# Choosing evacuation engines and the place of the output scaling by a beam search, and packing a short group's chunks two to a bank

## The chip, the cores and the metric

The kernel runs on one core of one Trainium2 chip. The metric is the device time of one execution in microseconds (us); "span" is the time from the first to the last instruction in the profile of one execution, about 2 us less. All runs told of here were with a granted TensorE clock between 0.996 and 1.0. Short names: PE is TensorE's matmul row, PEld its weight loads, DVE is VectorE, ACT is ScalarE, POOL is GpSimd, SP is SyncE.

## The reference, cut to what matters

```python
# x: (4, 12480, 128), inducing: (32, 128), w_in: (128, 2048), w_out: (2048, 128), alpha: (2048,)
def mab(q, kv):                       # attention with softmax, scale 1/sqrt(128)
    a = softmax(scale * (q @ kv.T))
    return a @ kv
h   = mab(inducing, x)                # 32 summary rows for each of 4 batches
y   = mab(x, h)                       # back to all rows; 49,920 rows of 128
u   = y @ w_in
out = (max(u, 0) + alpha * min(u, 0)) @ w_out
```

The kernel uses two identities. `y @ w_in` is (softmax weights) @ (h @ w_in), so the first layer's matmul contracts over 32 and not 128. And max(u,0) + alpha min(u,0) is (1 - alpha) relu(u) + alpha u; the second term is linear, so a small matmul, called here the linear term, adds it to the same accumulator. The softmax division is left to the very end, one scaling of the finished rows.

## The kernel before: the parts that the argument touches

Rows go in groups of 512; a batch has 24 full groups and one short group of 192 rows. A group's second layer accumulates in one of two PSUM banks (`accs`), chosen by the group's parity. The other six PSUM banks are a ring. A group takes four *fills*. Fill j: four matmuls, each on its own 32 rows of TensorE, write four ring banks (128x512); ACT or DVE *evicts* each bank with a relu into the SBUF tile `gt`; one fill later, 16 matmuls (`mm2`) multiply `gt` by the second-layer weights.

```python
    def fill(st, g, j):
        ...
        for r in range(4):
            ps = bank()                                   # next bank of the ring of six
            mm(ps[:, :w], st.hW[32*r : 32*r+32, j, :], rep[32*r : 32*r+32, :w])
            banks.append((ps, (ring_n[0] - 1) % RING))
        if j == 2:
            linear(st, lin_groups(st.b, g))               # even g: for groups g and g+1
        ca, cd = w * 0.75 + 96, w * 1.04 + 68             # modelled ns on ACT, DVE
        ...
        for r, (ps, i) in enumerate(banks):               # greedy: whichever ends first
            ta, td = max(clk["A"], ready) + ca, max(clk["D"], ready) + cd
            if ta <= td: ...  nc.scalar.activation(out=gt[:, r, :w], in_=ps[:, :w], func=RELU)
            else:        ...  nc.vector.tensor_relu(gt[:, r, :w], ps[:, :w])

    def mm2(st, g, j, gt, done):                          # runs after the NEXT fill's matmuls
        ...                                               # 16 matmuls into accs[(st.b*NG + g) % 2]
        if j == NJ - 1 and st.b * NG + g > 0:
            finish(st, g)                                 # the scaling, on DVE

    def linear(st, groups):                               # groups = [g, g+1]
        for k in range(NB):
            for r, g in enumerate(groups):
                mm(accs[(st.b*NG + g) % 2][:pp, k, :], st.rep[g][32*r : ...], st.hA[32*r : ...],
                   start=(r == 1 and k == 0), ...)        # r == 1 restarts the bank of g-1 and g+1
    def finish(st, g):                                    # ob = acc * 1/den, then the output DMA
        ...

    for b, g, j in fills:
        gt, done = fill(states[b], g, j)
        for fn in tasks.pop((b * NG + g, j), []):         # the next batch's work, and this one's
            fn()                                          # b_scores, b_den; most take a ring bank
        if prev is not None:
            mm2(*prev)
        prev = (states[b], g, j, gt, done)
```

So group g-1's last `mm2` comes after fill 0 of group g, its scaling is evicted on DVE during fill 1, and, for even g, the linear term in fill 2 restarts that very bank for group g+1. I call fills 0 to 3 of a group its first to fourth fill.

The softmax here doesn't subtract the row's maximum and nothing guards it: scores larger than these inputs give would overflow.

Of the kernel before, what the change touches and what calls it, by code (L numbers as in the profile page):

```python
# [15 lines left out]
P = 128  # L16
NB = 4
GRP = P * NB
NQ = 4
# [5 lines left out]
def kernel(  # L25
# [62 lines left out]


    clk = {"P": 0.0, "A": 0.0, "D": 0.0}  # L90
    free = [0.0] * RING

    def bank():
        i = ring_n[0] % RING
        ring_n[0] += 1
        clk["P"] = max(clk["P"], free[i])
        return ring[i]

    def spent(e, ns, release=True):
        clk[e] = max(clk[e], clk["P"] + 100) + ns  # L100
        if release:
            free[(ring_n[0] - 1) % RING] = clk[e] + 100
# [82 lines left out]
    def e_xpose_pe(st, u):  # L185
        e1 = st.e1.pop(u)
        tp = bank()[:].bitcast(bf16)
        if u < NS:
            e1T = work.tile([P, NB, P], bf16, name="e1T", tag="e1T")
            for j in range(NB):  # L190
# [3 lines left out]
            pin(nc.vector.tensor_copy(  # L194
                out=e1T[:].rearrange("p j m -> p (j m)"), in_=tp[:, : NB * P]
            ))
# [11 lines left out]
    def a_scores(st, u, by_dma=True):  # L208
# [24 lines left out]
        clk["P"] += 320  # L233
        spent("A", 680)
# [5 lines left out]
    def a_accum(st, u):  # L240
# [3 lines left out]
        clk["P"] += 240  # L244
# [22 lines left out]
        spent("D", 220)  # L267
# [38 lines left out]
    def b_scores(st, s):  # L306
# [16 lines left out]
        clk["P"] += 320  # L323
        spent("A", 490)
# [31 lines left out]
    def b_den(st, s):  # L356
        e2 = st.e2.pop(s)
        ps = bank()
        clk["P"] += 240
        spent("D", 250)  # L360
# [16 lines left out]

    def shape_of(g):
        return (P, NB) if g < NS * NQ else (PR, JR)

    def fill(st, g, j):
        pp, nb = shape_of(g)
        w = pp * nb
# [3 lines left out]
        for r in range(4):  # L387
            ps = bank()
            mm(
                ps[:, :w], st.hW[32 * r : 32 * r + 32, j, :], rep[32 * r : 32 * r + 32, :w]  # L390
            )
            banks.append((ps, (ring_n[0] - 1) % RING))
        if j == 2:
            linear(st, lin_groups(st.b, g))
        ca, cd = w * 0.75 + 96, w * 1.04 + 68
        ready = clk["P"] + 150 + w * 0.42
        clk["P"] = ready - 50 + (240 if j == 2 and lin_groups(st.b, g) else 0)
        done = ready
        for r, (ps, i) in enumerate(banks):
            ta, td = max(clk["A"], ready) + ca, max(clk["D"], ready) + cd  # L400
            if ta <= td:
                clk["A"] = free[i] = ta
                pin(nc.scalar.activation(out=gt[:, r, :w], in_=ps[:, :w], func=RELU))  # L403
            else:
                clk["D"] = free[i] = td
                pin(nc.vector.tensor_relu(gt[:, r, :w], ps[:, :w]))  # L406
            free[i] += 150
            done = max(done, free[i])
        return gt, done

    def mm2(st, g, j, gt, done):
        pp, nb = shape_of(g)
        acc = accs[(st.b * NG + g) % 2]
        clk["P"] = max(clk["P"], done) + 4 * nb * 57
        begun = g % 2 == 1 and st.b + g > 1
        for r in range(4):
            c = r * NJ + j
            for k in range(nb):
                mm(
                    acc[:pp, k, :], gt[:, r, k * pp : (k + 1) * pp], W1[:, c, :],  # L420
                    start=(j == 0 and r == 0 and k == 0 and not begun), stop=False,
                    skip_group_check=True,
                )
        if j == NJ - 1 and st.b * NG + g > 0:
            finish(st, g)
# [9 lines left out]
    def linear(st, groups):  # L435
        for k in range(NB):
            for r, g in enumerate(groups):
                pp, nb = shape_of(g)
                if k < nb:
# [4 lines left out]
                        start=(r == 1 and k == 0), stop=False, skip_group_check=True,  # L444
                    )

    def finish(st, g):
        pp, nb = shape_of(g)
# [9 lines left out]
        spent("D", nb * C * 1.04 + 68, release=False)  # L458
# [12 lines left out]
    for u in order[:2]:  # L471
# [9 lines left out]
    for u in order[2:]:  # L481
# [106 lines left out]
    fills = [(b, g, j) for b in range(B) for g in range(NG) for j in range(NJ)]  # L588
# [3 lines left out]
    def at(slot, fn, j=1):  # L592
        tasks.setdefault((slot, j), []).append(fn)
# [5 lines left out]
    for q in range(1, NQ):  # L599
        at(0, lambda q=q: b_scores_pe(st, 0, q), q)  # L600
# [78 lines left out]
```

## Time and profile before

| | before |
|---|---|
| time, median (all its runs, those beside the experiments too, lie between 616.7 and 618.6) | 617.5 us |
| span of the profiled run | 615.2 us |
| first fill starts / last matmul starts | 29.5 / 609.1 us |
| PE, DVE, ACT busy | 97%, 85%, 81% |

These lines are from the page of the kernel before: the span, the busy times, the chain that ended last by engine, and three groups of instructions (busy us, mean ns of one, then idle time before them and its releaser).

```profile
span 615.2 us, 21846 instructions
PE 598.9 (97%) x9180; PEld 436.7 (71%) x9180; DVE 524.2 (85%) x935; ACT 500.8 (81%) x994; POOL 89.0 (14%) x151
...
PE 95%; DVE 0%; ACT 0%; issue 0%
...
L105 PEld LDWEIGHTS <-gt 128*128 128x128 bf16 x6272 | 352.9, 98 | 83.0 <-issue 73.6
...
L403 ACT ACTIVATE gt<-ring_82 128x512 bf16<-128x512 f32 (+1 forms) x164 | 95.6, 583 | 12.2 <-ACT gt L403 7.9
...
L406 DVE TENSOR_SCALAR gt<-ring_83 128x512 bf16<-128x512 f32 (+1 forms) x128 | 84.3, 659 | 12.9 <-PE ring_85 L105 6.0
```

Read this with care. PE is 97% busy, but the Trainium skill ("Trainium Kernel Development and Optimization", Reading a trace) calls matmul busy time a bad metric for how close a kernel is to roofline (the limit of the hardware), because matmuls are pipelined. A matmul's record is drawn 0.22 us long where the next one starts 0.056 us later, so short waits vanish beneath overlapping records. The waits in TensorE have to be read from the *starts* of consecutive matmul records. Done over the whole trace, from 36 us on, an undisturbed fill takes 1.33 us, and in 105 of 392 fills one of the four matmuls starts more than 0.05 us late; all late starts together are 22.2 us (I call these bank waits; with other thresholds for "late" the sum moves by up to 1.4 us).

One such place, in the timeline of the kernel before (start us, length us, engine, line, operation, output<-inputs, count): the second fill of an even group, its scaling, and the third fill with the linear term.

```profile
503.37 0.38 PE L105 MATMUL ring_85<-rep,hW 32*128 32x512 bf16 x1
503.37 0.39 PE L105 MATMUL ring_86<-rep,hW 32*128 32x512 bf16 x1
...
503.76 0.68 DVE L455 TENSOR_TENSOR ob<-acc_87,rd 128x512 f32<-128x512 f32 x1
503.84 0.60 ACT L403 ACTIVATE gt<-ring_85 128x512 bf16<-128x512 f32 x1 [0.24 <-ACT gt L403]
504.33 0.59 ACT L403 ACTIVATE gt<-ring_86 128x512 bf16<-128x512 f32 x1
504.36 0.68 DVE L406 TENSOR_SCALAR gt<-ring_81 128x512 bf16<-128x512 f32 x1
...
504.70 0.38 PE L105 MATMUL ring_85<-rep,hW 32*128 32x512 bf16 x1
...
504.98 0.37 PE L105 MATMUL ring_86<-rep,hW 32*128 32x512 bf16 x1
504.98 0.23 PE L105 MATMUL acc_88<-hA,rep 32*128 32x128 bf16 x1
504.98 0.22 PE L105 MATMUL acc_87<-hA,rep 32*128 32x128 bf16 x1
...
505.31 1.07 PE L105 MATMUL acc_88<-W_169,gt 128*128 128x128 bf16 x16
...
506.31 0.38 PE L105 MATMUL ring_81<-rep,hW 32*128 32x512 bf16 x1
```

The scaling (the DVE line with `ob`) comes first on DVE; ACT takes tile one at 503.84 and tile two, `ring_86`, at 504.33 to 504.92. The next fill wants `ring_86` again: its fourth matmul starts at 504.98, 0.28 us after the third. The linear term follows at once. It uses the same 32-row tiles of TensorE (row groups) as the fill's first two matmuls, and behind a fill that is not late its first matmul starts only some time after the fill's fourth; behind one that is 0.27 us late, as here, it starts after 0.006 us. So a late fill hides this second wait, the *row-group wait*. From the second fill's start to the fourth's: 506.31 - 503.37 = 2.94 us. Two fills of which one has the linear term would take about 2.87 without bank waits (an estimate from fills of this trace that are not late: 1.33 and 1.54), so here the late fill costs little; in odd groups, without a linear term, a third fill that is 0.27 us late takes 1.58 to 1.60 us and not 1.33, so there all of it is lost.

### The profile page before, as it was taken

Reading aid. Unit: us, or ns where it says so; the run is one execution under the profiler, and the core shown is the slowest. Engines: PE = TensorE matmul, PEld = TensorE weight load, DVE = VectorE, ACT = ScalarE, POOL = GpSimd, SP = SyncE. Lnnn points to the kernel's source line nnn. Section 1 sums busy time; section 2 is a strip of 40 time slices with the busy share of each in tenths; the row PEclk is TensorE's granted clock in tenths of the full one; section 3 lists DMA queues with packets and bytes.
Section 4 is the critical chain, followed back from the end, with each engine's and each line's share of the span. In section 5 each row is a group of like instructions: output and inputs, shape, how many; then the busy total and the mean of one; then the engine's idle time right before and its main releaser. Section 6 shows DMA issues by size and latency. Waiting matters only on the chain.

```text
span 615.2 us, 21846 instructions
## 1 busy us (share of the span) xinstructions
PE 598.9 (97%) x9180; PEld 436.7 (71%) x9180; DVE 524.2 (85%) x935; ACT 500.8 (81%) x994; POOL 89.0 (14%) x151
## 2 busy tenths in 40 slices
PE   5799999999999999999999999999999999999996
PEld 4577777777777777777777777777777777777774
DVE  4688888889988888888988888888898888888885
ACT  2678888888888888888878888888888888888884
POOL 7241112101011111111011112110101011011010
PEclk9999999999999999999999999999999999999999
DMA  9824879652125598763122588864121221221211
GB/s 141 173 69 99 185 154 180 152 113 86 51 84 129 125 177 184 144 151 87 58 96 91 111 169 168 171 154 122 62 81 54 86 95 53 80 96 46 87 56 43
DMA packets 87458, 68.66 MB, mean 112 GB/s; under 512 B 53200, under 2 KB 80736, under 8 KB 87360
## 3 DMA queue, kind: packets, MB, share of 16 engines
q0 software_dynamic: 21456, 39.82, 26.2%
q1 hardware_dynamic: 65904, 27.45, 20.4%
q8 instruction: 72, 1.18, 0.8%
q14 instruction: 26, 0.21, 0.1%
HBM read 39.94 MB, written 28.62 MB: 111 GB/s over the span
## 4 chain that ended last, share of the span: by engine, by line
PE 95%; DVE 0%; ACT 0%; issue 0%
PE acc_87 L105 32%; PE acc_88 L105 32%; PE ring_82 L105 5%; PE ring_86 L105 5%; PE ring_84 L105 5%; PE ring_83 L105 5%; PE ring_81 L105 5%; PE ring_85 L105 5%; DVE gt L406 0%; ACT rep L342 0%; ACT gt L403 0%; PE ring_83 L543 0%; PE ring_81 L543 0%; DVE e1T L194 0%; DVE ob L455 0%
## 5 line engine op out<-in xcount | busy, mean ns | idle before, releaser
L105 PEld LDWEIGHTS <-gt 128*128 128x128 bf16 x6272 | 352.9, 98 | 83.0 <-issue 73.6
L105 PE MATMUL acc_87<-W_169,gt 128*128 128x128 bf16 (+1 forms) x3136 | 209.8, 220 | 0.0
L105 PE MATMUL acc_88<-W_169,gt 128*128 128x128 bf16 (+1 forms) x3136 | 209.6, 220 | 0.0
L461 POOL DMA_DIRECT2D out_dram<-ob x99 | 53.6, 541 | 501.6 <-DVE ob L455 482.2
L403 ACT ACTIVATE gt<-ring_86 128x512 bf16<-128x512 f32 (+1 forms) x159 | 92.2, 580 | 17.3 <-ACT gt L403 9.8
L403 ACT ACTIVATE gt<-ring_82 128x512 bf16<-128x512 f32 (+1 forms) x164 | 95.6, 583 | 12.2 <-ACT gt L403 7.9
L403 ACT ACTIVATE gt<-ring_84 128x512 bf16<-128x512 f32 (+1 forms) x151 | 88.5, 586 | 20.0 <-ACT gt L403 15.0
L105 PE MATMUL ring_84<-rep,hW 32*128 32x512 bf16 (+1 forms) x273 | 103.5, 379 | 0.0
L105 PE MATMUL ring_83<-rep,hW 32*128 32x512 bf16 (+1 forms) x273 | 103.0, 377 | 0.0
L105 PE MATMUL ring_81<-rep,hW 32*128 32x512 bf16 (+1 forms) x270 | 102.0, 378 | 0.7 <-ACT gt L403 0.4
L406 DVE TENSOR_SCALAR gt<-ring_81 128x512 bf16<-128x512 f32 (+1 forms) x139 | 91.3, 657 | 13.2 <-PE ring_83 L105 4.8
L105 PE MATMUL ring_86<-rep,hW 32*128 32x512 bf16 (+1 forms) x269 | 101.4, 377 | 0.1
L403 ACT ACTIVATE gt<-ring_85 128x512 bf16<-128x512 f32 x149 | 89.3, 599 | 12.3 <-ACT gt L403 8.4
L105 PE MATMUL ring_82<-rep,hW 32*128 32x512 bf16 (+1 forms) x258 | 97.4, 378 | 0.0
L105 PE MATMUL ring_85<-rep,hW 32*128 32x512 bf16 (+1 forms) x257 | 97.2, 378 | 0.0
L406 DVE TENSOR_SCALAR gt<-ring_83 128x512 bf16<-128x512 f32 (+1 forms) x128 | 84.3, 659 | 12.9 <-PE ring_85 L105 6.0
L406 DVE TENSOR_SCALAR gt<-ring_84 128x512 bf16<-128x512 f32 x122 | 83.6, 685 | 13.5 <-PE ring_86 L105 5.3
L403 ACT ACTIVATE gt<-ring_83 128x512 bf16<-128x512 f32 (+1 forms) x145 | 86.8, 598 | 10.3 <-ACT gt L403 7.5
L403 ACT ACTIVATE gt<-ring_81 128x512 bf16<-128x512 f32 x131 | 78.9, 602 | 19.4 <-ACT gt L403 13.0
L406 DVE TENSOR_SCALAR gt<-ring_85 128x512 bf16<-128x512 f32 (+1 forms) x108 | 72.1, 667 | 12.5 <-issue 5.4
L406 DVE TENSOR_SCALAR gt<-ring_86 128x512 bf16<-128x512 f32 x110 | 75.2, 684 | 7.4 <-ACT gt L403 3.0
L406 DVE TENSOR_SCALAR gt<-ring_82 128x512 bf16<-128x512 f32 x94 | 64.5, 687 | 10.1 <-issue 3.4
(299 smaller groups left out, 377.9 us busy)
## 6 DMA issues: line engine op xcount, KB each, us to landing
out_dram<-ob POOLq DMA_DIRECT2D x96, 256.0 KB, 2.6
rep<-e2d SPq DMA_DIRECT2D x92, 128.0 KB, 3.3
xn<-in_x_dram POOLq DMA_DIRECT2D x18, 512.0 KB, 6.0
xn<-in_x_dram POOLq DMA_DIRECT2D x12, 256.0 KB, 7.7
w_out_f<-in_moe_w_out_dram POOLq DMA_DIRECT2D x1, 1024.0 KB, 13.5
w_in_b<-in_moe_w_in_dram POOLq DMA_DIRECT2D x1, 512.0 KB, 11.4
xT<-xn SPq DMA_TRANSPOSE x18, 4.7
out_dram<-ob POOLq DMA_DIRECT2D x3, 96.0 KB, 2.0
```

Of the source, the lines that this page charges most:

```text
L105: return pin(nc.tensor.matmul(o, lhsT, rhs, start=start, stop=stop, **kw))
L403: pin(nc.scalar.activation(out=gt[:, r, :w], in_=ps[:, :w], func=RELU))
L406: pin(nc.vector.tensor_relu(gt[:, r, :w], ps[:, :w]))
L461: pin((nc.sync if last_one else nc.gpsimd).dma_start(out=out[t0 : t0 + pp * nb, :].rearrange("(p j) c -> p j c", j=nb), in_=ob[:pp, :nb, :],))
```

## The change

Its intent is to avoid such waits by planning ahead. In place of the greedy rule, a beam search over a clock model, at build time, picks for each fill a bit mask (which tiles ACT evicts) and a position (before which tile the scaling stands in DVE's order). Besides, the short group is done in two fills of two chunks to a bank instead of four, two background tasks move to other fills (a_scores and a_accum, the next batch's attention scores and the weighted sums made with them), and at the start a third load is issued before the identity is built and one copy goes from DVE to ACT.

```diff
     def fill(st, g, j):
...
+        bits, pos = plan[st.b * NG + g, j]
+        for r, ps in enumerate(banks):
+            if r == pos:
+                flush()                       # the scaling held from the last mm2
+            if bits >> r & 1:
                 pin(nc.scalar.activation(out=gt[:, r, :w], in_=ps[:, :w], func=RELU))
             else:
-                clk["D"] = free[i] = td
                 pin(nc.vector.tensor_relu(gt[:, r, :w], ps[:, :w]))
+        flush()
...
-        return (P, NB) if g < NS * NQ else (PR, JR)
+        return (P, NB, 1) if g < NS * NQ else (PR, JR, 2)       # two chunks to a bank
...
-            finish(st, g)
+            held.append((st, g))
...
-                at(k + 5, lambda n=n, u=u: a_scores(states[n], u))
-                at(k + 8, lambda n=n, u=u: a_accum(states[n], u))
+                at(k + 5, lambda n=n, u=u: a_scores(states[n], u), 0, (320, "A", 680))
+                at(k + 8, lambda n=n, u=u: a_accum(states[n], u), 2, (240, "D", 220))
...
+    def make_plan():                          # cut to its core
+        for i, (b, g, j) in enumerate(fills):
+            lin = 240 if j == 2 // cp and lin_groups(b, g) else 0
+            for P_, A_, D_, free, done, hist in beam:
+                for r in range(4):
+                    P_ = max(P_, free[idx[r]])                  # the ring banks
+                ready = P_ + 240 + w * 0.42
+                P1 = P_ + 105 + w * 0.42 + lin                  # the linear term: 240 ns
+                for bits in range(1, 15):
+                    for pos in (0, 2, 4) if ended else (4,):
+                        ...                                     # scaling: d = max(d, P_) + 600
+                        late = sum(max(0, x - p) for x in f)
+                        rank = p + 0.1 * (a + d - 2 * p) + 0.1 * late
+            # the best 60 that differ are kept
```

More of the change, by code (lines that the diff above doesn't have):

```diff
@@ L86 @@
     ring_n = [0]
-    clk = {"P": 0.0, "A": 0.0, "D": 0.0}
-    free = [0.0] * RING
     def bank():
-        i = ring_n[0] % RING
+        t = ring[ring_n[0] % RING]
         ring_n[0] += 1
-        clk["P"] = max(clk["P"], free[i])
-        return ring[i]
-    def spent(e, ns, release=True):
-        clk[e] = max(clk[e], clk["P"] + 100) + ns
-        if release:
-            free[(ring_n[0] - 1) % RING] = clk[e] + 100
+        return t
     def mm(o, lhsT, rhs, start=True, stop=True, **kw):
@@ L193, in e_xpose_pe @@
                 ))
-            pin(nc.vector.tensor_copy(
-                out=e1T[:].rearrange("p j m -> p (j m)"), in_=tp[:, : NB * P]
-            ))
+            dst = e1T[:].rearrange("p j m -> p (j m)")
+            if u in order[-3:-2]:
+                pin(nc.scalar.copy(out=dst, in_=tp[:, : NB * P]))
+            else:
+                pin(nc.vector.tensor_copy(out=dst, in_=tp[:, : NB * P]))
         else:
@@ L232, in a_scores @@
                 ))
-        clk["P"] += 320
-        spent("A", 680)
         if by_dma:
@@ L243, in a_accum @@
         ps = bank()
-        clk["P"] += 240
         if u < NS:
@@ L265, in a_accum @@
             ))
-        spent("D", 220)
     def h_sum(st):
@@ L322, in b_scores @@
         pin(nc.sync.dma_start(out=st.d[s][:], in_=e2[:]))
-        clk["P"] += 320
-        spent("A", 490)
         st.e2[s] = e2
@@ L358, in b_den @@
         ps = bank()
-        clk["P"] += 240
-        spent("D", 250)
         if s < NS:
@@ L378, in shape_of, with flush @@
     def shape_of(g):
-        return (P, NB) if g < NS * NQ else (PR, JR)
+        return (P, NB, 1) if g < NS * NQ else (PR, JR, 2)
+    held = []
+    def flush():
+        while held:
+            finish(*held.pop())
     def fill(st, g, j):
-        pp, nb = shape_of(g)
-        w = pp * nb
+        pp, nb, cp = shape_of(g)
+        t = pp * nb
+        w = t * cp
         rep = st.rep[g]
@@ L388, in fill @@
             ps = bank()
-            mm(
-                ps[:, :w], st.hW[32 * r : 32 * r + 32, j, :], rep[32 * r : 32 * r + 32, :w]
-            )
-            banks.append((ps, (ring_n[0] - 1) % RING))
-        if j == 2:
-            linear(st, lin_groups(st.b, g))
-        ca, cd = w * 0.75 + 96, w * 1.04 + 68
-        ready = clk["P"] + 150 + w * 0.42
-        clk["P"] = ready - 50 + (240 if j == 2 and lin_groups(st.b, g) else 0)
-        done = ready
-        for r, (ps, i) in enumerate(banks):
-            ta, td = max(clk["A"], ready) + ca, max(clk["D"], ready) + cd
-            if ta <= td:
-                clk["A"] = free[i] = ta
+            for i in range(cp):
+                mm(
+                    ps[:, i * t : (i + 1) * t],
+                    st.hW[32 * r : 32 * r + 32, j * cp + i, :],
+                    rep[32 * r : 32 * r + 32, :t],
+                )
@@ L403, in fill @@
+            banks.append(ps)
+        lin = j == 2 // cp and lin_groups(st.b, g)
+        if lin:
+            linear(st, lin)
+        bits, pos = plan[st.b * NG + g, j]
[3 more added lines that the diff above has]
+            if bits >> r & 1:
                 pin(nc.scalar.activation(out=gt[:, r, :w], in_=ps[:, :w], func=RELU))
             else:
-                clk["D"] = free[i] = td
                 pin(nc.vector.tensor_relu(gt[:, r, :w], ps[:, :w]))
-            free[i] += 150
@@ L408, in fill, with mm2 @@
-            done = max(done, free[i])
-        return gt, done
-    def mm2(st, g, j, gt, done):
-        pp, nb = shape_of(g)
+        flush()
+        return gt
+    def mm2(st, g, j, gt):
+        pp, nb, cp = shape_of(g)
         acc = accs[(st.b * NG + g) % 2]
-        clk["P"] = max(clk["P"], done) + 4 * nb * 57
-        begun = g % 2 == 1 and st.b + g > 1
+        begun = (g % 2 == 1 and st.b + g > 1) or cp > 1
         for r in range(4):
-            c = r * NJ + j
-            for k in range(nb):
-                mm(
-                    acc[:pp, k, :], gt[:, r, k * pp : (k + 1) * pp], W1[:, c, :],
-                    start=(j == 0 and r == 0 and k == 0 and not begun), stop=False,
-                    skip_group_check=True,
-                )
-        if j == NJ - 1 and st.b * NG + g > 0:
-            finish(st, g)
+            for i in range(cp):
+                c = r * NJ + j * cp + i
+                for k in range(nb):
+                    k0 = (i * nb + k) * pp
+                    mm(
+                        acc[:pp, k, :], gt[:, r, k0 : k0 + pp], W1[:, c, :],
+                        start=(j == 0 and r == 0 and i == 0 and k == 0 and not begun),
+                        stop=False, skip_group_check=True,
+                    )
+        if j == NJ // cp - 1 and st.b * NG + g > 0:
+            held.append((st, g))
@@ L437, in linear @@
             for r, g in enumerate(groups):
-                pp, nb = shape_of(g)
+                pp, nb, cp = shape_of(g)
                 if k < nb:
@@ L443, in linear @@
                         st.hA[32 * r : 32 * r + 32, :],
-                        start=(r == 1 and k == 0), stop=False, skip_group_check=True,
+                        start=((r == 1 or cp > 1) and k == 0), stop=False, skip_group_check=True,
                     )
     def finish(st, g):
-        pp, nb = shape_of(g)
+        pp, nb, _ = shape_of(g)
         acc = accs[(st.b * NG + g) % 2]
@@ L457, in finish @@
         ))
-        spent("D", nb * C * 1.04 + 68, release=False)
         t0 = st.b * N + g * GRP
@@ L470 @@
     st = new_batch(0)
-    for u in order[:2]:
+    for u in order[:3]:
         a_load(st, u, pieces=2)
@@ L480 @@
     nc.sync.dma_start(out=al_f[:], in_=moe_alpha.rearrange("(k p) -> k p", p=P))
-    for u in order[2:]:
+    for u in order[3:]:
         a_load(st, u, pieces=2)
@@ L585, with at @@
     warm(8)
-    fills = [(b, g, j) for b in range(B) for g in range(NG) for j in range(NJ)]
+    fills = [(b, g, j) for b in range(B) for g in range(NG)
+             for j in range(NJ // shape_of(g)[2])]
     states = {0: st}
     tasks = {}
-    def at(slot, fn, j=1):
-        tasks.setdefault((slot, j), []).append(fn)
+    def at(slot, fn, j=1, cost=None):
+        tasks.setdefault((slot, j), []).append((fn, cost))
     def late_finish():
@@ L599 @@
     for q in range(1, NQ):
-        at(0, lambda q=q: b_scores_pe(st, 0, q), q)
-    at(1, lambda: b_den_pe(st, 0, 0), 0)
-    at(1, w_amat)
-    at(1, lambda: h_linear(st), 2)
+        at(0, lambda q=q: b_scores_pe(st, 0, q), q, (240, "A", 480))
+    at(1, lambda: b_den_pe(st, 0, 0), 0, (130, "D", 250))
+    at(1, w_amat, 1, (950, "D", 250))
+    at(1, lambda: h_linear(st), 2, (80, "D", 250))
     at(1, late_finish, 3)
@@ L606 @@
     for q in range(1, NQ):
-        at(q, lambda q=q: b_den_pe(st, 0, q))
+        at(q, lambda q=q: b_den_pe(st, 0, q), 1, (130, "D", 250))
     for b in range(B):
@@ L612 @@
             g = base + s * NQ - 4
-            at(g, lambda b=b, s=s: b_scores(states[b], s), 3)
+            at(g, lambda b=b, s=s: b_scores(states[b], s), 3, (320, "A", 490))
             at(g + 1, lambda b=b, s=s: b_rep(states[b], s), 3)
-            at(g + 2, lambda b=b, s=s: b_den(states[b], s), 3)
+            at(g + 2, lambda b=b, s=s: b_den(states[b], s), 3, (130, "D", 250))
         if b + 1 < B:
@@ L626 @@
                 at(k + 3, lambda n=n, u=u: a_xpose(states[n], u))
-                at(k + 5, lambda n=n, u=u: a_scores(states[n], u))
-                at(k + 8, lambda n=n, u=u: a_accum(states[n], u))
+                at(k + 5, lambda n=n, u=u: a_scores(states[n], u), 0, (320, "A", 680))
+                at(k + 8, lambda n=n, u=u: a_accum(states[n], u), 2, (240, "D", 220))
             k = base + NG - 5
             at(k, lambda n=n: h_sum(states[n]))
-            at(k, lambda n=n: h_den(states[n]), 3)
@@ L632 @@
-            at(k + 1, lambda n=n: h_transpose(states[n]))
-            at(k + 1, lambda n=n: h_weights(states[n]), 3)
-            at(k + 2, lambda n=n: b_scores(states[n], 0))
-            at(k + 2, lambda n=n: h_linear(states[n]), 3)
-            at(k + 3, lambda n=n: b_rep(states[n], 0), 0)
-            at(k + 3, lambda n=n: b_den(states[n], 0))
+            at(k, lambda n=n: h_den(states[n]), 3, (250, "D", 500))
+            at(k + 1, lambda n=n: h_transpose(states[n]), 1, (300, "D", 250))
@@ new lines @@
+            at(k + 1, lambda n=n: h_weights(states[n]), 3, (320, "D", 600))
+            at(k + 2, lambda n=n: b_scores(states[n], 0), 1, (320, "A", 490))
+            at(k + 2, lambda n=n: h_linear(states[n]), 3, (80, "D", 250))
+            at(k + 3, lambda n=n: b_rep(states[n], 0), 0)
+            at(k + 3, lambda n=n: b_den(states[n], 0), 1, (130, "D", 250))
+    def make_plan():
+        beam = [(0.0, 0.0, 0.0, (0.0,) * RING, None, None)]
+        at_bank = ring_n[0]
+        ended = False
+        for i, (b, g, j) in enumerate(fills):
+            pp, nb, cp = shape_of(g)
+            w = pp * nb * cp
+            ca, cd = w * 0.75 + 96, w * 1.04 + 68
+            lin = 240 if j == 2 // cp and lin_groups(b, g) else 0
+            costs = [c for _, c in tasks.get((b * NG + g, j), []) if c]
+            idx = [(at_bank + r) % RING for r in range(4)]
+            nxt = []
+            for P_, A_, D_, free, done, hist in beam:
[5 more added lines that the diff above has]
+                    for pos in (0, 2, 4) if ended else (4,):
+                        a, d, f, dn = A_, D_, list(free), []
+                        for r in range(4):
+                            if ended and r == pos:
+                                d = max(d, P_) + 600
+                            if bits >> r & 1:
+                                a = t = max(a, ready) + ca
+                            else:
+                                d = t = max(d, ready) + cd
+                            f[idx[r]] = t + 200
+                            dn.append(t + 200)
+                        if ended and pos == 4:
+                            d = max(d, P_) + 600
+                        p, k = P1, at_bank + 4
+                        for pe, e, ns in costs:
+                            p = max(p, f[k % RING]) + pe
+                            if e == "A":
+                                a = t = max(a, p + 100) + ns
+                            else:
+                                d = t = max(d, p + 100) + ns
+                            f[k % RING] = t + 100
+                            k += 1
+                        if done is not None:
+                            n0, c0, d0 = done
+                            for r in range(4):
+                                p = max(p, d0[r]) + c0 * n0 * 57
+                            p += 85
+                        late = sum(max(0, x - p) for x in f)
+                        rank = p + 0.1 * (a + d - 2 * p) + 0.1 * late
+                        nxt.append((rank, p, a, d, tuple(f), (nb, cp, dn), (hist, bits, pos)))
+            nxt.sort(key=lambda x: x[0])
+            beam, seen = [], set()
+            for x in nxt:
+                key = tuple(
+                    int(max(y - x[1], -50) / 50)
+                    for y in (x[2], x[3], *x[4], *x[5][2])
+                )
+                if key not in seen:
+                    seen.add(key)
+                    beam.append(x[1:])
+                    if len(beam) == 60:
+                        break
+            at_bank += 4 + len(costs)
+            if i:
+                b1, g1, j1 = fills[i - 1]
+                ended = j1 == NJ // shape_of(g1)[2] - 1 and b1 * NG + g1 > 0
+        plan, hist = {}, beam[0][5]
+        for b, g, j in reversed(fills):
+            hist, bits, pos = hist
+            plan[b * NG + g, j] = (bits, pos)
+        return plan
@@ L639 @@
+    plan = make_plan()
     prev = None
     for b, g, j in fills:
-        gt, done = fill(states[b], g, j)
-        for fn in tasks.pop((b * NG + g, j), []):
+        gt = fill(states[b], g, j)
+        for fn, _ in tasks.pop((b * NG + g, j), []):
             fn()
@@ L645 @@
             mm2(*prev)
-        prev = (states[b], g, j, gt, done)
+        prev = (states[b], g, j, gt)
     mm2(*prev)
+    flush()
     assert not tasks, tasks
```

## The prediction

> **What bounds it.** TensorE: PE 97% busy on the page, 95% of the chain of waits. The Trainium skill ("Trainium Kernel Development and Optimization", Reading a trace) calls matmul busy time a bad metric for pipelining; this trace agrees: the PE row hides waits. So I took start-to-start gaps of matmul records. An undisturbed fill (four 32-row matmuls of 512 columns, then 16 second-layer matmuls) takes 1.33 us: 0.32 + 15 x 0.056 + 0.15 (timeline: 303.89 to 305.22). But between the four matmuls of a fill, starts are late by 22.2 us in all, in 105 of 392 steady fills: they wait for a PSUM bank. No second-layer matmul waits visibly. By position in a group of four fills: third fill 12.6 us, first of odd groups 4.6, last of odd groups 3.1, second 2.4.
>
> The cause shows in the timeline: a 128x512 eviction takes 0.60 us on ACT (0.48 apart) and 0.685 on DVE (0.605 apart), and starts about 0.46 us after its fill. In each group's second fill the old greedy rule places the output scaling (0.68 us, DVE) first and evicts ACT, ACT, DVE, ACT. Tile two is then free at +1.55 us, but the next fill wants it at +1.34: about 0.26 us lost.
>
> **What the change does.** Same matmuls; ACT evicts 878 of 1536 full tiles (before 863): loads hardly move. The plan (read from a build) makes the second fill ACT, DVE, scaling, ACT, ACT (83 of 96; the rest too evict on DVE first); ACT, ACT, DVE, DVE is used only where a task follows; a_scores and a_accum move to other fills. Bank waits should fall from 22.2 to about 3 us. About 3.5 us come back: after an undelayed fill the linear matmul waits 0.16 us for its row group, which the late fills hid.
>
> Short groups: four fills of 0.78 us become two of about 1.32: about 0.5 x 4 = 1.9 us saved.
>
> **What it adds.** In even groups the third fill is followed by the linear term, whose second matmul restarts the accumulator that the scaling is reading. The built program has that wait; the search's model has not. Scaling first ends at about +1.1, harmless. Behind a DVE eviction: +0.46 + 0.605 + 0.68 = +1.75, seen at PE at +1.80; the linear matmul could start at +1.50. So about 0.30 us of new TensorE wait in some 44 even groups: +13 us. All of it is critical.
>
> Startup: a third load precedes the identity; the last x load still gates this part (wait at 21.9 us). About 0.
>
> **Sum.** 615.2 - 22.2 + 3.5 + 3 - 1.9 + 13 = 610.6 us span, 1 us for the search's errors, 2.3 from span to time: about 614 us. Range 604 to 619. Faster by over 2%: 0.14; within 2%: 0.84; slower by over 2%: 0.02.
>
> **What would show it.** Right: the late starts within fills drop below 6 us; instead, gaps of about 0.3 us between the first and second linear matmul in even groups, released by the scaling; short groups about 2.6 us each. DVE and ACT busy nearly unchanged. Wrong: no gap there (then about 601 us), or bank waits still above 10 us (then above 616).
>
> **What would make it wrong.** The scaling starting earlier than my sum, the 0.3 us giving slack that would have been lost anyway, or evictions drifting from the modelled 0.48 and 0.60 us, so the plan misses.

## The result, and the profile after

| | before | after |
|---|---|---|
| time, median of 6 runs each, same chip | 617.51 us | 617.38 us |
| ratio of the means, 95% interval | | 0.9995 (0.9983 to 1.0008) |
| span of the profiled run | 615.2 us | 615.7 us |
| last matmul starts | 609.1 us | 608.8 us |
| bank waits (starts late within a fill) | 22.2 us | 7.1 us |
| gaps over 0.05 us between first and second linear matmul | 5, 0.4 us in all | 46, 12.6 us in all |

Ratios here and below are the mean time of one kernel's fast runs over that of the other's fast runs of the same rounds, so not quite the ratio of the quoted medians. The last two rows are computed from the starts of all matmul records of each trace; the bank waits from 36 us to 605 us.

The time is the same. These are the lines of the page after that answer to those shown of before.

```profile
span 615.7 us, 21682 instructions
PE 596.0 (97%) x9179; PEld 436.4 (71%) x9180; DVE 520.3 (84%) x899; ACT 507.6 (82%) x998; POOL 89.0 (14%) x151
...
L94 PEld LDWEIGHTS <-gt 128*128 128x128 bf16 x6272 | 352.5, 98 | 73.6 <-issue 67.7
...
L395 ACT ACTIVATE gt<-ring_82 128x512 bf16<-128x512 f32 (+1 forms) x159 | 95.4, 600 | 14.8 <-ACT gt L395 9.7
...
L397 DVE TENSOR_SCALAR gt<-ring_83 128x512 bf16<-128x512 f32 (+1 forms) x122 | 83.5, 685 | 12.0 <-PE ring_84 L94 5.6
```

Nothing on the page tells that 15 us of waits have gone and others have come: the shares are the same. (The page's chain follows only 4% of the span in this trace, so it is no help either.) The timeline tells. This is an even group in the kernel after, the same three steps as above.

```profile
67.62 0.38 PE L94 MATMUL ring_86<-rep,hW 32*128 32x512 bf16 x1
67.63 0.39 PE L94 MATMUL ring_81<-rep,hW 32*128 32x512 bf16 x1
...
68.09 0.60 ACT L395 ACTIVATE gt<-ring_86 128x512 bf16<-128x512 f32 x1 [0.24 <-ACT gt L395]
68.14 0.69 DVE L397 TENSOR_SCALAR gt<-ring_81 128x512 bf16<-128x512 f32 x1
68.59 0.59 ACT L395 ACTIVATE gt<-ring_82 128x512 bf16<-128x512 f32 x1
68.75 0.68 DVE L446 TENSOR_TENSOR ob<-acc_88,rd 128x512 f32<-128x512 f32 x1
...
68.96 0.39 PE L94 MATMUL ring_81<-rep,hW 32*128 32x512 bf16 x1
...
69.18 0.21 PE L94 MATMUL acc_87<-hA,rep 32*128 32x128 bf16 x1
...
69.48 0.21 PE L94 MATMUL acc_88<-hA,rep 32*128 32x128 bf16 x1
...
69.79 1.07 PE L94 MATMUL acc_87<-W_169,gt 128*128 128x128 bf16 x16
...
70.79 0.38 PE L94 MATMUL ring_82<-rep,hW 32*128 32x512 bf16 x1
```

Now DVE takes tile two (`ring_81`) first and is done with it at 68.83, so the next fill's fourth matmul starts on time at 68.96: the bank wait is gone. But the scaling of `acc_88` runs from 68.75 to 69.43, and the second linear matmul, which restarts `acc_88`, starts only at 69.48, 0.30 us after the first. From the second fill's start to the fourth's: 70.79 - 67.62 = 3.17 us, 0.23 more than in the example before. Odd groups have no linear term; there a bank wait that is gone is a plain gain.

### The profile page after: what moved, and what is told of

Read it like the earlier page. It is cut to its first block, busy times and chain, and to the rows that moved or that the text cites. A ratio compares the mean times of both kernels' runs of the same rounds, so it can differ in the third digit from the quotient of the medians.

```text
span 615.7 us, 21682 instructions
## 1 busy us (share of the span) xinstructions
PE 596.0 (97%) x9179; PEld 436.4 (71%) x9180; DVE 520.3 (84%) x899; ACT 507.6 (82%) x998; POOL 89.0 (14%) x151
## 5 line engine op out<-in xcount | busy, mean ns | idle before, releaser
L395 ACT ACTIVATE gt<-ring_84 128x512 bf16<-128x512 f32 (+1 forms) x162 | 96.9, 598 | 18.2 <-ACT gt L395 14.6
L395 ACT ACTIVATE gt<-ring_82 128x512 bf16<-128x512 f32 (+1 forms) x159 | 95.4, 600 | 14.8 <-ACT gt L395 9.7
L395 ACT ACTIVATE gt<-ring_86 128x512 bf16<-128x512 f32 (+1 forms) x149 | 89.2, 599 | 13.3 <-ACT gt L395 8.8
L395 ACT ACTIVATE gt<-ring_81 128x512 bf16<-128x512 f32 (+1 forms) x143 | 85.7, 599 | 15.5 <-ACT gt L395 11.6
L395 ACT ACTIVATE gt<-ring_85 128x512 bf16<-128x512 f32 x147 | 88.2, 600 | 11.4 <-ACT gt L395 7.8
L395 ACT ACTIVATE gt<-ring_83 128x512 bf16<-128x512 f32 (+1 forms) x142 | 84.9, 598 | 11.6 <-ACT gt L395 6.5
L397 DVE TENSOR_SCALAR gt<-ring_83 128x512 bf16<-128x512 f32 (+1 forms) x122 | 83.5, 685 | 12.0 <-PE ring_84 L94 5.6
L397 DVE TENSOR_SCALAR gt<-ring_81 128x512 bf16<-128x512 f32 (+1 forms) x117 | 80.1, 685 | 12.4 <-PE ring_83 L94 3.8
L397 DVE TENSOR_SCALAR gt<-ring_86 128x512 bf16<-128x512 f32 x113 | 77.6, 687 | 13.3 <-PE ring_81 L94 8.2
L397 DVE TENSOR_SCALAR gt<-ring_85 128x512 bf16<-128x512 f32 (+1 forms) x113 | 77.1, 683 | 11.2 <-PE ring_81 L94 4.4
L397 DVE TENSOR_SCALAR gt<-ring_84 128x512 bf16<-128x512 f32 x102 | 70.1, 688 | 12.1 <-PE ring_85 L94 6.2
L397 DVE TENSOR_SCALAR gt<-ring_82 128x512 bf16<-128x512 f32 x99 | 68.0, 687 | 11.2 <-PE ring_83 L94 5.6
## 6 DMA issues: line engine op xcount, KB each, us to landing
w_in_b<-in_moe_w_in_dram POOLq DMA_DIRECT2D x1, 512.0 KB, 12.2
```

The lines of the kernel that those rows point to most:

```text
L395: pin(nc.scalar.activation(out=gt[:, r, :w], in_=ps[:, :w], func=RELU))
L397: pin(nc.vector.tensor_relu(gt[:, r, :w], ps[:, :w]))
```

## The experiments

All outputs are right. Each run was timed beside the kernel before on the same chip. The medians of the kernel before were 617.28, 617.23, 617.10 and 617.31 us. A summary first; the last three columns are from the matmul starts of each trace.

| run | time us | ratio to before | bank waits us | linear gaps, us | last matmul us |
|---|---|---|---|---|---|
| after | 617.38 | 0.9995 | 7.1 | 46, 12.6 | 608.8 |
| e1 linear term one fill later, plan kept | 601.37 | 0.9743 | 4.9 | 5, 0.3 | 592.5 |
| e2 the same, plan searched for it | 603.05 | 0.9771 | 5.1 | 5, 0.3 | 594.2 |
| e3 the search is told of the wait | 605.99 | 0.9814 | 11.6 | 6, 0.5 | 597.3 |
| e4 scaling first, engines searched | 609.49 | 0.9871 | 15.8 | 5, 0.3 | 600.9 |
| e5 the two tasks back in place | 612.75 | 0.9925 | 8.7 | 28, 6.2 | 604.2 |
| e6 before, linear term one fill later | 617.93 | 1.0011 | 18.2 | 5, 0.4 | 610.2 |
| e7 before, scaling behind a DVE eviction | 622.09 | 1.0079 | 20.4 | 28, 5.0 | 613.7 |
| e8 before, short groups changed alone | 614.32 | 0.9951 | 20.9 | 5, 0.3 | 605.5 |
| e9 as e1, one pattern by hand, no search | 603.22 | 0.9776 | 4.5 | 5, 0.3 | 592.9 |
| e10 as e2, three constants measured | 602.65 | 0.9772 | 4.0 | 5, 0.3 | 592.4 |
| e11 e1 again | 601.45 | 0.9753 | 4.9 | 5, 0.3 | 592.4 |
| e12 after, b_den one fill earlier | 612.63 | 0.9924 | 3.9 | 40, 11.5 | 604.2 |
| e13 e1, last two outputs from SP | 598.38 | 0.9692 | 4.9 | 5, 0.3 | 592.6 |

### e1: take the wait away, keep the plan

```diff
-        lin = j == 2 // cp and lin_groups(st.b, g)
+        lin = j == (3 if cp == 1 else 1) and lin_groups(st.b, g)
```

> The changed kernel with its plan untouched; only the linear matmuls of a pair of groups are issued one fill later (fourth fill of the even group, not third), where the scaling that they wait for (ends about 1.75 us after the second fill starts) is long done. My theory (the linear term waits for the scaling that the search pushed behind a DVE eviction): the 0.30 us gaps between first and second linear matmul vanish, about 44 x 0.30 = 13 us, and the b_den waits (3.8 us) shrink as the linear term now lengthens that fill: about 602 us (599 to 606). Rival A (ACT and DVE together are the limit, a wait taken away comes back as a bank wait): 615 to 618 us, with waits within fills up by 10 us or more.

Measured 601.37 us, 16.0 less than the kernel after, as the theory said. The timeline of e1, an even group (equal records are drawn together here, and the names have no numbers):

```profile
66.83 0.40 PE L94 MATMUL ring<-rep,hW 32*128 32x512 bf16 x4
...
67.95 0.68 DVE L446 TENSOR_TENSOR ob<-acc,rd 128x512 f32<-128x512 f32 x1
68.15 0.40 PE L94 MATMUL ring<-rep,hW 32*128 32x512 bf16 x4
68.48 1.07 PE L94 MATMUL acc<-W,gt 128*128 128x128 bf16 x16
...
69.48 0.40 PE L94 MATMUL ring<-rep,hW 32*128 32x512 bf16 x4
69.70 0.39 PE L94 MATMUL acc<-hA,rep 32*128 32x128 bf16 x8
...
71.12 0.40 PE L94 MATMUL ring<-rep,hW 32*128 32x512 bf16 x4
```

The second and third fills now start 1.32 and 1.33 us before their successors, and the eight linear matmuls, which need the scaled bank, run 0.39 us in one piece, more than a microsecond after the scaling's end. The same instructions run on every engine: rival A (ACT and DVE are the limit) falls, for the time fell and bank waits did not come back: in all they fell to 4.9 us. By the starts, 12.3 us of the gain are the gaps; another 2.2 are bank waits (most of those after b_den, the task that computes a block's softmax divisors, went; smaller ones came in 24 fourth fills) and 2.2 row-group waits (16.7 together; the last matmul comes 16.3 us sooner).

### e2: the search is told the new place

```diff
-            lin = 240 if j == 2 // cp and lin_groups(b, g) else 0
+            lin = 240 if j == (3 if cp == 1 else 1) and lin_groups(b, g) else 0
```

> As the run before, but the search is told the new place of the linear term, so its plan is made for it. Theory: 600 us (597 to 605), waits within fills under 6 us. Rival A: 615 to 618. If the plan matters much, this is 3 us or more below the run with the old plan; I expect less than 3.

603.05 us: within the range, but 1.7 us *above* the run whose plan was made for the wrong place. The new plan has third fills of even groups with bank waits of 2.9 us in all (26 of 48), where it lets the scaling start first and DVE evict tile two after it. In the model the scaling starts when its fill starts; in the trace before it never starts sooner than 0.1 us after, and in nine of ten cases between 0.1 and 0.5 (median 0.33). In sum the bank waits are nearly those of e1 (5.1 against 4.9 us). What differs is where they stand: e1 has 2.2 us of them in 24 fourth fills, where they hide the linear term's row-group wait, and e2 has none there. That wait is 8.1 us in all in e1 and 10.5 in e2; no other kind of transition between matmuls grew by more than 0.2 us. So the plan that the search found for the right place loses to one made for the wrong place, by a wait that its model does not have.

### e3: the search is told of the wait

```diff
+                if lin and cp == 1:
+                    P1 = max(P1, fe_ + 450)          # fe_: the scaling's end, carried in the state
...
-                                d = max(d, P_) + 600
+                                d = fe = max(d, P_) + 600
```

> The changed kernel with the linear term where it was, but the search's clock model has the missing wait: the linear term is not done before the scaling's end plus 450 ns. Theory: the search trades, in even groups, the 0.30 us wait for a bank wait of about 0.26 us of which the row-group wait of the linear term (0.21) hides most: about 607 us (603 to 612). Rival A: 615 to 618. Rival B (the search's other model errors are what costs): no gain either.

605.99 us, as expected: one missing term in the model was worth 11.4 us. The plan's remedy was better than mine: in 43 of 48 even groups it puts the third ACT eviction into the *first* fill, so that DVE is free early, the scaling can go first, and the bank wait behind it is 0.1 us and not 0.26 (4.2 us in 40 third fills).

### e4: less freedom for the search

```diff
-                    for pos in (0, 2, 4) if ended else (4,):
+                    for pos in (0,) if ended else (4,):
```

> The changed kernel with the scaling's place fixed first in its fill (as before the change), the engines still searched. Theory: no linear wait (13 us less) but the second tile of the second fill comes free at about +1.55 us instead of +1.15, so bank waits at the third fill come back in even and odd groups: 0.26 x about 90 = 23 us, less 9 to 10 us of row-group wait hidden in even groups: 614 to 619 us, waits within fills 20 us or more.

A miss: 609.49 us, 4.5 below the lower end of my range. I had assumed that the masks would stay; the search found the same remedy as in e3 (third ACT eviction one fill earlier) for 47 of the 48 even groups and 26 of the odd ones, and its third fills wait 0.1 us each (9.3 us in 87 fills), not 0.26. What follows is worth keeping: with one freedom *taken away* the search gave a kernel 8 us faster than with it, because the freedom was priced by a model that lacked its cost.

### e5: the two moved tasks put back

```diff
-                at(k + 5, ... a_scores(states[n], u), 0, (320, "A", 680))
-                at(k + 8, ... a_accum(states[n], u), 2, (240, "D", 220))
+                at(k + 5, ... a_scores(states[n], u), 1, (320, "A", 680))
+                at(k + 8, ... a_accum(states[n], u), 1, (240, "D", 220))
```

> The changed kernel with a_scores and a_accum back in the second fill, where they were before the change, the plan searched again. Theory: a_accum then stands between the scaling and the linear term in 18 even groups and hides the 0.30 us wait there: 18 x 0.30 = 5.4 us less, with some bank waits back where five banks are used: 611 to 615 us. Rival C (the moved tasks cost nothing either way): 616 to 618.

612.75 us, as expected. The gaps in the linear term fall from 46 to 28, by 18: in the trace none of the 18 groups in which the a_accum of a full block of rows stands before the linear term again has a gap. In time they fall from 12.6 to 6.2 us. So the change's move of a_accum, harmless in the model, bared the wait in 18 groups.

### e6: the same move of the linear term in the kernel before

```diff
-        if j == 2:
+        if j == (3 if nb == NB else 2):
             linear(st, lin_groups(st.b, g))
```

(and the same in the greedy rule's clock)

> The kernel before the change with the linear matmuls one fill later, nothing else. There the linear term never waited for the scaling, so the gain of the same move in the changed kernel (16 us) must not show. b_den waits shrink by 2 to 4 us, the row-group wait no longer hides behind bank waits (3 us more): 614 to 619 us. If it falls to 605 or lower, the linear term's place is good in itself and my account of the changed kernel is wrong.

617.93 us, no gain: bank waits fell by 4.0 us, and the linear term's wait for its 32-row tile, no longer hidden behind bank waits, rose from 4.7 to 10.6 us. The linear term's new place is therefore not good in itself; it was worth 16 us in the kernel after, where the wait for the scaling is.

### e7: the wait put into the kernel before

```diff
                 pin(nc.vector.tensor_relu(gt[:, r, :w], ps[:, :w]))
+                while held:
+                    finish(*held.pop())       # in even groups: scaling behind the first DVE tile
```

(masks and clock as in the kernel before)

> The kernel before the change, same engine for each tile, but in even groups the scaling stands behind the first DVE eviction of its fill, as the search puts it: the suspected wait is put into the old kernel. Theory: gaps of about 0.2 to 0.3 us in the linear term in some 27 even groups without a_accum in between, bank waits nearly as they were: 5 to 8 us slower, 621 to 626 us. Rival (the place of the scaling is harmless): 616 to 619.

622.09 us, 4.9 slower than before, with 28 gaps of 5.0 us in all where there had been 5. Two lines of its timeline, the third fill of an even group and its linear term:

```profile
495.79 0.65 PE L105 MATMUL ring<-rep,hW 32*128 32x512 bf16 x4
496.07 0.59 PE L105 MATMUL acc<-hA,rep 32*128 32x128 bf16 x8
```

Both waits stand here one after the other: the fill is stretched by its bank wait (0.65 against 0.40 us in e1), and the linear term by the scaling, which ended at 496.24 (0.59 against 0.39).

### e8: the short groups alone

```diff
-        return (P, NB) if g < NS * NQ else (PR, JR)
+        return (P, NB, 1) if g < NS * NQ else (PR, JR, 2)      # and the loops over cp that go with it
```

> The kernel before the change with only the short groups changed (two chunks to a bank, two fills in place of four), greedy rule kept. The traces show the four short fills going from 3.73 to 2.69 us, of which 0.45 us is second-layer work shifted to the next fill: 0.6 us a batch, 2.4 us in all: 614.5 to 616 us.

614.32 us, 2.9 less than before (0.9951, interval 0.9938 to 0.9963), a little more than expected. In the traces a batch's short group takes 2.69 us in place of 3.73, of which 0.45 (eight second-layer matmuls of 0.056) moves into the next fill; bank waits are 1.3 us less too. So the short groups alone gained 2.9 us, and the kernel after, which has them as well, took 3.1 us more than e8: the rest of the change (the search, the moved tasks, the start) made it slower.

### e9, e10, e11: is the search needed, and do better constants help?

e9 drops the search for one pattern:

```diff
-    plan = make_plan()
+    plan = {(b * NG + g, j): (13, 2) if j == 1 and g < NS * NQ else (5, 4)
+            for b, g, j in fills}
```

> No search: linear term in the fourth fill as in the first run, and one pattern written by hand: every second fill of a full group ACT, DVE, scaling, ACT, ACT; every other fill ACT, DVE, ACT, DVE. If the gain comes from that one spot plus the place of the linear term: 600 to 604 us. If the search's fitting to single fills matters: above 605, with new waits where tasks take a fifth bank.

e10 takes e2 and puts in what the traces show:

```diff
-                                a = t = max(a, ready) + ca
+                                a = max(a, ready) + ca
+                                t = a + 170                        # was: free at t + 200
...
-                                d = t = max(d, ready) + cd
+                                d = max(d, ready) + cd
+                                t = d + 130
...
-                                d = max(d, P_) + 600
+                                d = max(d, P_ + 180) + 600
```

> Linear term in the fourth fill, plan searched with three constants taken from the traces: a bank is free 170 ns (ACT) or 130 ns (DVE) after the modelled end in place of 200, the scaling starts no sooner than 180 ns after its fill's start, and it may stand at any place in its fill. The bank waits of 2.9 us at the third fills of even groups in the earlier search (scaling modelled too early) should go: 600 to 602 us, 1 to 3 us below that run.

> The kernel of the first run once more, on the same chip as the two beside it, for comparison: 601.4 us (600.9 to 602).

e9 took 603.22 us, e10 602.65, e11 601.45 (single runs 600.7 to 605.7, e10 and e11 scattering most). On TensorE the three end together: last matmul at 592.9, 592.4 and 592.4 us. (e10's trace is of its fastest run, 1.2 us below its median, so its place among the three is not sure.) So one pattern written by hand does as well as the search, within half a microsecond. e10 missed its expectation on time by 0.7 us; its bank waits did fall by 1.0 us against e2 (those in third fills of even groups from 2.9 to 0.3), but it does not beat e1 either. Of the 1.9 us between the spans of e9 and e11, 1.3 lie after the last matmul; e13 takes that up.

### e12: the bank waits that the change left

```diff
-            at(g + 2, lambda b=b, s=s: b_den(states[b], s), 3, (130, "D", 250))
+            at(g + 2, lambda b=b, s=s: b_den(states[b], s), 2, (130, "D", 250))
```

> The changed kernel with b_den moved from the fourth to the third fill of its group, where the linear term already lengthens the fill; plan searched again. The remaining bank waits of the changed kernel are 7.1 us, of which 3.8 us (23 waits of 0.17) stand right after b_den, as many as before the change: I had counted on the search to remove them. If they come from a fill that needs a fifth bank without the time to free it, they go: 613 to 615.5 us (less than the full 3.8, as three of the six fills of a batch then hold a_accum as well). If the search could have removed them where they are: no change, 617.

612.63 us, 4.7 less than the kernel after, just below the expected range. Bank waits fell from 7.1 to 3.9 us, and those after b_den from 3.8 us (23 of them) to 0.5. b_den takes a fifth ring bank but TensorE for only 0.11 us; in its old place the next fill needed three of the four banks just filled, and the search found no choice that frees three in time. The linear gaps fell too, from 46 of 12.6 us to 40 of 11.5: the new plan puts the scaling first in 9 even groups, and none of these has a gap. So of the 4.7 us about 3.2 are bank waits, 1.1 gaps and 1.0 row-group waits (by the starts; together 5.3).

### e13: the end of the span

```diff
-        last_one = (st.b, g) == (B - 1, NG - 1)
+        last_one = st.b == B - 1 and g >= NG - 2          # output from SP, not GpSimd
```

(on top of e1)

> The kernel of the first run (601.4 us) with the output of the last two groups, not only of the last, issued from the SP queue. In all traces the span ends with a GpSimd drain that lasts 7.2 to 7.3 us from its last output issue (the last full group's), whatever TensorE does: TensorE ended 0.25 us sooner in the changed kernel and the span 0.5 us later. Theory: without that issue the drain starts about 5 us earlier and the SP's last output ends the span: about 2.5 us less, 598.5 to 599.5 us. Rival (the landing of the last output ends it): no change, 601.4.

598.38 us, 3.0 below e1: what the theory said, a little more of it (0.1 us below its range). The instruction records show why (drain and issue, start us and length):

```
            last GpSimd output issue   GpSimd drain     span ends
before      607.26                     607.24, 7.17     615.20
after       607.77                     607.75, 7.21     615.75
e1          591.44                     591.42, 7.28     599.47
e9          593.18                     593.16, 7.17     601.11
e13         587.25                     587.23, 7.09     596.64
```

In the first four, the span ends 7.9 to 8.0 us after the start of GpSimd's last output issue, the output of the last full group, whatever TensorE does after it. In the kernel after, that issue comes 0.51 us later than before: this is the half microsecond by which its span is longer although its last matmul is 0.25 us earlier. It is not that the scaling is held back. In both kernels it starts 0.04 us after the last matmul into its bank ends (at 606.24 before, 606.75 after); TensorE reaches that matmul 0.51 us later. What TensorE then gains, 0.76 us in the short group still to come, lies after the issue and cannot shorten the span. e8, which holds no scaling back, has the same tail: 7.0 us from the last matmul to the end, against 6.1 before and 6.9 after. In e9 the scaling is held back, behind the evictions of its fill, and starts 1.35 us after that matmul ends; this is most of the 1.6 us between the spans of e9 and e1. The scalings of the last full group and the output issues in the two timelines, before and then after:

```profile
606.28 0.69 DVE L455 TENSOR_TENSOR ob<-acc_87,rd 128x512 f32<-128x512 f32 x1 [0.29 <-PE acc_87 L105]
...
607.26 0.54 POOL L461 DMA_DIRECT2D out_dram<-ob  x1 [4.89 <-DVE gt L406]
...
609.80 0.32 SPq L461 DMA_DIRECT2D out_dram<-ob  x1
```

```profile
606.79 0.69 DVE L446 TENSOR_TENSOR ob<-acc_87,rd 128x512 f32<-128x512 f32 x1 [0.36 <-PE acc_87 L94]
...
607.77 0.54 POOL L451 DMA_DIRECT2D out_dram<-ob  x1 [3.78 <-DVE ob L446]
...
609.55 0.32 SPq L451 DMA_DIRECT2D out_dram<-ob  x1
```

e13 is the fastest kernel, 3.1% below the kernel before (0.9692, interval 0.9679 to 0.9705).

## Why the prediction was right or wrong

The forecast was 614 us, 3.5 less than before; measured is 617.4, no change. The range and the verdict (within 2%) held, the mechanism was right, and the forecast gain was not there. The step that failed is the size of one term, "Bank waits should fall from 22.2 to about 3 us": they fell to 7.1, and so the prediction's own test for it (below 6 us) failed too. By its terms, in us:

| step of the prediction | predicted | measured | from |
|---|---|---|---|
| bank waits fall from 22.2 to about 3 | -19.2 | -15.1 | to 7.1, matmul starts |
| linear matmul waits for its row group, no longer hidden | +3.5 | +5.6 | fill-to-linear starts, 4.7 to 10.3 in all |
| linear term waits for the scaling | +13 | +12.2 | 46 gaps, 12.6, less 0.4 before |
| short groups | -1.9 | -2.4 | 4 x (3.73 - 2.69 - 0.45); e8: -2.9 in time |
| end of the span after the last matmul | 0 | +0.8 | 615.7 - 608.8 against 615.2 - 609.1 |
| sum | -4.6 | +1.1 | span: +0.5; the prediction then added 1 us for errors of the search |

(The last measured column adds up to half a microsecond more than the span shows; small items, like 0.2 us of other matmul transitions and the rounding of these classes, make up the rest.)

- **Right: what bounds the kernel and where.** TensorE's order of work with its bank waits; the wait of 0.26 us at third fills is in the timeline before (0.28 there) and is all but gone after.
- **Right: the hidden cost.** "So about 0.30 us of new TensorE wait in some 44 even groups" became 46 gaps with a total of 12.6 us. e1 takes the wait away and the gain appears; e6 shows that the same edit gives nothing where the wait isn't; e7 puts the wait into the old kernel and pays for it; e3 teaches it to the search. This cause is shown, not only argued.
- **Wrong, mis-sized: "Bank waits should fall from 22.2 to about 3 us."** They fell to 7.1. In the trace before, 3.8 us of the waits stood after b_den, in every one of its 23 places, and I credited the search with removing them. They are still there after, 3.8 us in 23 places: the fill after b_den needs a third bank that is evicted too late, and the search found no plan that avoids it. e12 brings them to 0.5 us by moving b_den, and the time falls by 4.7, of which they are the greater part. This is the largest term of the miss.
- **Wrong, mis-sized: "the linear matmul waits 0.16 us for its row group".** I read 0.16 off fills that were themselves 0.055 us late. In the kernel after the wait behind an undisturbed fill is 0.216 us, which makes 5.6 us of it, not 3.5.
- **Wrong, left out: the end.** I took the tail as unchanged. It is set by GpSimd's last output issue (shown by e13), which comes before the last short group is done, so that the saving in that group did not reach the end of the span (e8 has the same tail).
- **The start** was told right: the first fill starts at 29.6 us after, 29.5 before.

So three errors, all in the same direction, of 4.1, 2.1 and 0.8 us (two smaller ones, 0.8 and 0.5, went the other way), on a forecast that was the small difference of large terms: -19, +16. A forecast of that make deserves to be called "no change, up to 5 us either way".

The Trainium skill ("TensorEngine Tiling (Array Packing)", PSUM Bottleneck) warns that after row tiling the PSUM evacuation may become the bottleneck, and advises to use both ScalarE and VectorE. The two engines can keep up (a tile each 0.48 us on ACT and 0.605 on DVE; side by side, an estimate from these two, four tiles in 1.07 us, for a fill of 1.33 us on TensorE), so what costs is not their load (85% and 81% before, 84% and 82% after) but the order in which they give banks back. The page on "PSUM — Partial Sum Buffer" (PSUM bank collisions raise a hardware error) asks that PSUM be guarded by semaphores per bank and quadrant (32 partitions), or more simply per bank; the wait of the linear term for the scaling is such a guard, between a DVE read and TensorE's next write of one bank (in the example after, the read ends at 69.43 and the write starts at 69.48). No run here left the guard out; only its place was moved.

## What to carry to other kernels

A build-time search optimises what its model has: before giving it a new freedom (here, where the scaling stands), list every semaphore wait that the freedom can lengthen and put each into the model, or the search will spend what it can't see (e3: one term, 11.4 us; e4: less freedom, 8 us better). When a change takes 15 us of waits away and the time stays, compare start-to-start gaps of the bounding engine by kind of transition: the new wait appears as one class that has grown. And time the parts of a change alone: here one part gained 2.9 us (e8), which the whole did not show. Moving the waiting work one slot later was better here than the other orders tried of the work it waits for (e1 against e3 and e4), and a fixed pattern then did as well on TensorE as the search (e9).

## What the Trainium skill lacked or had wrong

- No page that I read tells how to find TensorE waits shorter than a matmul's drawn length. "Perfetto Trace Analysis" (Tensor Engine Instruction; Identifying the Most-Contended Engine; Optimization Strategy) says that the end of a matmul is estimated and that matmul busy time is no measure; it sends the reader to weight-load busy time (PEld, 71% before and after, although bank waits fell from 22.2 to 7.1 us) and to gaps between slices, of which there are hardly any here (PE 97% busy in both). Gaps between *starts* show them.
- "TensorEngine Tiling (Array Packing)", Key Properties: tiles operate independently. Not said: how long a second matmul on the same row tile has to wait. Here it started 0.216 us after the last of a fill's four 512-column matmuls (kernel after, 46 of 48 cases within 0.002), and after 0.006 us when that one was 0.27 us late (kernel before).
- No page that I read gives a length for the drain with which GpSimd ends a program. Here it took 7.1 to 7.3 us in the five kernels of the table under e13, from its last output issue on, and in all but e13 it set the end of the span. It stands at the line of the program's own context (`with ... TileContext`), so it need not be one of the runtime's drains, which "VectorE: DVE Perf Modes" (The DRAIN you can't avoid) puts at about 12 ns.
